# The opening of a fused attention and Mish kernel: first group's maxima first, statistics on ScalarE, input kept whole, keys in two column tiles

## The chip, the cores and the metric

The kernel runs on one core of a Trainium2 chip. A core has TensorE (PE, with its weight loads listed apart as PEld), VectorE (DVE), ScalarE (ACT), GpSimd (POOL) and SyncE (SP), which here only issues DMAs. Every engine works through its own list of instructions in order and waits on semaphores of the others. The metric is the device time of one execution in microseconds (us); lower is better. Before the change it is 1585.07, the median of 3 runs (1584.73 to 1585.38).

## The reference

`x` is 1 x 2048 x 512. It is normalised row by row, then goes two ways, which are multiplied:

```python
xn = (x - mean(x)) / sqrt(var(x) + 1e-5)

# A: attention, 32 query heads of 16, one key head and one value head shared by all
q = (xn @ wq) split into 32 heads; k = xn @ wk; v = xn @ wv      # wk, wv: 512 x 16
p = softmax(q k^T * 16 ** -0.5)
s = concat(p @ v) @ wo

# B: dense, Mish, dense
h = xn @ w1 + b1                                                  # 512 x 1792
g = silu((h * tanh(softplus(h))) @ w2)                            # 1792 x 512

out = x + s * g
```

All arrays are float32.

## The kernel before

The 2048 rows are four *blocks* of 512 (`NC`, `C`), and each block four *tiles* of 128 rows; tile `t` is the `t % 4`-th of block `t // 4`. Products that need float32 accuracy on the fast path are made of three products of high and low parts (`TERMS`): a high part is the value rounded to the engine's fast format, the low part is the rest.

Attention is cut into 32 *units* `v` of 16 *steps*. A unit is four heads with the 512 queries of one block; a step takes one tile of 128 keys against them: four score products (`e`), an exponential each on ScalarE (into `pts`), and four value products (`pv`). The softmax needs the greatest score of every query row beforehand. So for every unit there are also 32 pairs of *maximum products* (`m`; the two of a pair are of two heads, a = 0 and 1, which lie in the upper and the lower 64 rows of PE's array): 128 queries against one block of 512 keys; VectorE reduces each to one column (`mb`). Pair `n` of a unit belongs to key block `n // 8`. When a unit's 32 pairs are done, `c_rows` makes *rows* of them (three small reductions, a 32x32 transpose) and eight DMAs write these rows into the unit's query tile `qt`, where they are subtracted by the score product itself. Unit 0 can therefore give no score before all of its 32 pairs are done, with the keys of all four blocks. The maxima run `LEAD` = 22 steps ahead of the scores: 44 pairs are made before the first score. A query product (`q_group`) makes eight heads, enough for two units; units 0 and 1 come from the first.

Beside the scores PE does the *extra* products (`xps`): the query products, the first dense layer (`m1_group`, from a weight tile `ws`), the second (`m2_groups`, tiles `wb`) and the output (`wo_groups`). Weights come by DMA into one of two *raw* buffers and are split there into high part (ScalarE in the opening, GpSimd later) and low part (GpSimd). The activation between the layers runs on ScalarE and GpSimd.

The *opening* is what stands ahead of the first score. A small planner at the end of the function builds it: tasks with an engine, a guessed duration (`us`), predecessors and a priority are placed one by one, always the one that can start first; where PE has a free moment it gets a pair of maxima ("M"), part of an extra product ("X") or a product that is thrown away (`warm`). The order that it writes down is then fixed for each engine. `E0` is the planner's guess of when the first score starts, and `X_US` how often an extra group may begin. The tasks are, for every block: statistics of its tiles on VectorE (`stats`: BN_STATS, BN_AGGR), the root of the variance (`norm_a` on VectorE, `norm_b` as Ln and Exp on ScalarE, `norm_c` on VectorE; blocks 2 and 3 together), scaling (`x_scale`: VectorE in block 0, ScalarE after), transposing on PE, copying from PSUM, and the product with `wk` and `wv` (`k_proj` into `kp`). Keys are then written to rows 0 to 47 of `ks` as high part (`k_high`, ScalarE) and low part (`k_low`, VectorE), and `k_move` copies them by DMA to rows 64 to 111, because the products of a = 1 read there. Only then can maxima of that block start.

The order of pairs in the opening is a table, `MSEQ`: eight pairs of unit 0, eight of unit 1, the other 24 of unit 0, then unit 1. While the row steps of unit 0 are pending, `m_ready` lets no pair through.

The transposed input of blocks 1 to 3 is split at once (`x_high2` on ScalarE, `x_low2` on GpSimd). Block 1 stays in SBUF, blocks 2 and 3 are stored split in DRAM (`xt_keep`) and come back later in four DMAs (`xt_loads`). Before that, `wbs` and `ot_all` are their homes, so the tiles of the second layer's weights come late.

Of the kernel before, what the change touches and what calls it, by code (L numbers as in the profile page):

```python
# [20 lines left out]
P = 128  # L21
# [14 lines left out]
E0 = 86.0  # L36
X_US = 13.0
# [21 lines left out]
MSEQ = ([(0, n) for n in range(8)] + [(1, n) for n in range(8)]  # L59
        + [(0, n) for n in range(8, 32)] + [(1, n) for n in range(8, 32)])  # L60


def m_need(v):

    return (40, 64)[v] if v < 2 else 32 * (v + 1)
# [59 lines left out]
def block_kernel(ctx: ExitStack, tc: tile.TileContext, x, wq, wk, wv, wo, w1, b1, w2, out):  # L125
# [34 lines left out]
    def pool_at(margin):  # L160
        t = step_of(busy[0]) + margin
        return max(t if lead else math.ceil(2 * t) / 2, step[0])
# [69 lines left out]

    def stats(t):
        st = sb.tile([P, 6], F32, tag="st", name=f"st{t}")
        dve.bn_stats(st, xin[divmod(t, 4)])
        dve.bn_aggr(mvs[:, t], st)

# [6 lines left out]
    def norm_a(z):  # L244
        dve.tensor_scalar(ve[:, z], mvs[:, z, 1], EPS, None, op0=ALU.add)
# [11 lines left out]

    def x_scale(t):
        x_ = xin[divmod(t, 4)]
        if t < 4:  # L260
            dve.tensor_scalar(x_, x_, rstd[:, t:t + 1], nbias[:, t:t + 1], op0=ALU.mult, op1=ALU.add)
        else:
            xn_scale(x_, x_, t)
# [3 lines left out]
    def x_transpose(t):  # L267
        c, tt = divmod(t, 4)
        xp_of[t] = ps_e.tile([P, NDT, P], F32, tag="e", name=f"xp{t}")
        for dt in range(NDT):  # L270
            pe.transpose(xp_of[t][:, dt], xin[c, tt][:, P * dt:P * (dt + 1)], ident)  # L271
# [22 lines left out]
    def x_high2(c, k):  # L294
        act.activation(xt_of[c][:, 0, 2 * k:2 * k + 2], xf_of[c][k], AF.Copy)

    def x_low2(c, k):
        sub(pool, xt_of[c][:, 1, 2 * k:2 * k + 2], xf_of[c][k], f(xt_of[c][:, 0, 2 * k:2 * k + 2]))

# [4 lines left out]

    def k_proj(c, dts):
        if 0 in dts:
            kp_of[c] = ps_v.tile([64, C], F32, tag="v", name=f"kp{c}")
        for dt in dts:
            if c > 0:
                pe.matmul(kp_of[c], wkf[:, dt], xf_of[c][dt // 2][:, dt % 2], start=(dt == 0), stop=(dt == 3))  # L310
                continue
            xt = xt_of[c]
            for i, (a, b) in enumerate(TERMS):
                pe.matmul(kp_of[c], wk3[:, a, dt], xt[:, b, dt], start=(dt + i == 0), stop=(dt == 3 and i == 2))

    def k_high(c):
        act.activation(ks[0:48, C * c:C * (c + 1)], kp_of[c][0:48], AF.Copy)

    def k_low(c):
        cs = slice(C * c, C * (c + 1))  # L320
        sub(dve, ks[0:16, cs], kp_of[c][0:16], f(ks[0:16, cs]))

    def k_move(c):
        cs = slice(C * c, C * (c + 1))
        sp.dma_start(f(ks[64:112, cs]), f(ks[0:48, cs]))

    def v_copy(c):
        vt_of[c] = sb.tile([P, C], F32, tag="xr", name=f"vt{c}", bufs=4)[0:32]
        act.activation(vt_of[c], kp_of[c][32:64], AF.Copy)
# [67 lines left out]

    def arrived(tag):
        k, n = todo[tag]
        if k >= RING[tag] and items[tag][k - RING[tag]].users:  # L400
# [3 lines left out]
    def home(tag, k):  # L404
        if tag == "wx":
            return (xt_of[NC] if k else new_xt(NC))[:, :, k]
        if tag == "wb":
# [38 lines left out]
    def load(tag):  # L446
# [4 lines left out]
        if n == len(its) or lead and tag == "wb" and n and now[0] < kept_at.get(3, 1e9):  # L451
            return
        it = its[n]
        taken = n >= RING[tag] and its[n - RING[tag]].users
        if taken and (tag != "ws" or kept.get(it.key)):
# [442 lines left out]
    def xt_keep(c, h):  # L898

        if h == 0:  # L900
            xt_kept[c] = dram.tile([P, 2, NDT, C], F32, tag=f"xt{c}", name=f"xtk{c}")
        sp.dma_start(xt_kept[c][:, h], f(xt_of[c][:, h]))

    def xt_loads(c, before):
        def part(k):
            if k == 0:
                new_xt(c)
            o = (slice(None), k // 2, slice(2 * (k % 2), 2 * (k % 2) + 2))
            done = sp_at(0.5) + 2
            sp.dma_start(f(xt_of[c][o]), xt_kept[c][o])  # L910
            if k == 3:
                xt_done[c] = math.ceil(done)

        def loads():
            for k in range(4):
                later(1 + 2 * k, lambda k=k: part(k))
# [16 lines left out]
    for c in range(NC):  # L933
        for k in range(3):
            a = take(2)
            if k == 1 and 1 <= c < NC - 1:
# [50 lines left out]
    m_next = [0, 0]  # L987

    def m_one(a, other=False):
        v, n = MSEQ[m_next[a]] if m_next[a] < 64 else divmod(m_next[a], 32)  # L990
# [26 lines left out]
    def c_rows(v):  # L1017
# [18 lines left out]
        def move():  # L1036
# [3 lines left out]
            for a in range(1, -1, -1):  # L1040
                r = 64 * a + 48
                for b in range(4):
                    sp_at(0.68)
                    sp.dma_start(f(q[r:r + 2]).rearrange("o p (t b n) -> b o (p t) n", b=4, n=32)[b],
# [107 lines left out]
    kept_at = {}  # L1152
# [48 lines left out]

    step[0] = (0.0 - E0) / STEP_US
    xat = {t: landed(DMA_US) for t in range(4)}
# [12 lines left out]
    new_xt(1)  # L1216
    tmp = ot_all.rearrange("p a h n -> p (a h) n").rearrange("p (h t) n -> p h t n", h=2)
    xt_of[2] = tmp
    xt_of[3] = wbs[:, 0:4].rearrange("p (h a) b n -> p h (a b) n", h=2)
# [8 lines left out]
    st = [task("DVE", 0.83, lambda t=t: stats(t), at=xat[t], prio=t // 4 * 2) for t in range(16)]  # L1228
    kv_done = None
    for c0, c1 in ((0, 1), (1, 2), (2, 4)):  # L1230
        z = slice(4 * c0, 4 * c1)
        na = task("DVE", 0.2, lambda z=z: norm_a(z), st[z], prio=c0 and 1)
        nb = task("ACT", 0.45, lambda z=z: norm_b(z), [na])
        nrm = task("DVE", 0.8, lambda z=z: norm_c(z), [nb], prio=2 * c0 and 1)
        for c in range(c0, c1):
            xs, his = [], []
            for t in range(4 * c, 4 * c + 4):
# [275 lines left out]
```

## Time and profile before

| what | value |
|---|---|
| time, median of 3 | 1585.07 us |
| profiled execution | 1585.32 us |
| its span | 1583.4 us |
| busy: PE, VectorE, ScalarE, GpSimd | 1566.4, 1342.0, 1295.1, 619.0 us |
| GpSimd busy, 0 to 100 us / 100 to 1500 us | 62.40 / 538.99 us |
| first maximum on VectorE | 30.30 us |
| first score product on PE | 91.19 us |

In the rows of a timeline the first number is the start in us from the span's start, the second the length of the row (several instructions in a row are merged, their number behind the x), then engine, line, operation, result <- operands and shapes; square brackets give idle time of the engine before the row and what ended it. SPq rows are issues of DMAs: their length is the time in which the queue was held by them. Matmuls of several row or column tiles overlap, so the lengths of PE rows can't be added. The granted TensorE clock is 1.00 in the opening and in the stage after it.

### The profile page before, as it was taken

To read this page: it belongs to the slowest core of one execution; us is meant where nothing else is said; L and a number is where in the kernel's file an instruction comes from. 1 tells how busy PE (TensorE), PEld (TensorE's weight loads), DVE (VectorE), ACT (ScalarE), POOL (GpSimd) and SP (SyncE) were. 2 spreads that over 40 slices of the span, in tenths; PEclk is the share of its full clock that TensorE was granted. 3 is DMA by queue.
4 is the path that set the end of the run, shared out by engine and by line. 5 is a ranking of instruction groups with operands and counts; after the bars stand their busy time and mean duration, and the time that the engine had idled before them with its cause. 6 is when DMAs were issued, how large, how long until landed. Compare 5 with 4: busy or idle time off the path is not lost.

```text
span 1583.4 us, 31224 instructions
## 1 busy us (share of the span) xinstructions
PE 1566.4 (99%) x11656; PEld 872.8 (55%) x11656; DVE 1342.0 (85%) x2299; ACT 1295.1 (82%) x2492; POOL 619.0 (39%) x626
## 2 busy tenths in 40 slices
PE   8999999999999999999999999999999999999998
PEld 5445555655555565565555556556555555655643
DVE  7988888888988988888898988888889999888821
ACT  5569889778899788877988888897788978888796
POOL 3788448338256111431624322163152323315021
PEclk9999999999999999999999999999999999999999
DMA  5333133124042215203113220332311213021200
GB/s 163 142 118 124 42 97 117 51 64 165 22 131 64 73 56 164 67 20 102 55 31 109 88 94 17 115 108 78 101 58 59 92 45 114 16 97 32 74 22 27
DMA packets 73542, 127.29 MB, mean 80 GB/s; under 512 B 21488, under 2 KB 35312, under 8 KB 72880
## 3 DMA queue, kind: packets, MB, share of 16 engines
q1 hardware_dynamic: 73392, 125.30, 25.2%
q8 instruction: 92, 1.51, 0.4%
q14 instruction: 58, 0.48, 0.1%
HBM read 76.36 MB, written 27.26 MB: 65 GB/s over the span
## 4 chain that ended last, share of the span: by engine, by line
PE 94%; ACT 2%; DVE 1%; POOL 1%; DMA 1%; SPq 0%; issue 0%; DVEq 0%; ACTq 0%; POOLq 0%
PE xps L118 42%; PE pv L1059 30%; PE m L1001 12%; PE e L973 6%; PE xps L114 2%; ACT pts L978 1%; PE kp L310 1%; DMA rawwb<-in_dram 1%; PE wop L114 0%; DVE mb L1005 0%; PE warm L1292 0%; POOL wbs L171 0%; DMA pts<-in_dram 0%; SPq L1077 0%; PE xp L271 0%
## 5 line engine op out<-in xcount | busy, mean ns | idle before, releaser
L1005 DVE TENSOR_REDUCE mb<-m 128x1 f32<-128x512 f32 x2048 | 1266.1, 681 | 169.9 <-PE m L1001 113.1
L978 ACT ACTIVATE pts<-e 128x512 f32<-128x512 f32 x2042 | 1062.3, 607 | 221.8 <-PE e L973 156.0
L1001 PE MATMUL m<-ks,qt 48*128 48x512 f32 (+1 forms) x2048 | 839.5, 425 | 1.1 <-DVE mb L1005 0.8
L973 PE MATMUL e<-qt,ks 64*128 64x512 f32 x2048 | 748.5, 408 | 1.8 <-ACT pts L978 1.7
L1059 PE MATMUL pv<-pts,vaug 128*32 128x512 f32 x4084 | 531.0, 603 | 0.0
L1001 PEld LDWEIGHTS m<-ks,qt 48*128 48x128 f32 (+1 forms) x2048 | 366.4, 185 | 114.4 <-DVE mb L1005 62.0
L973 PEld LDWEIGHTS e<-qt,ks 64*128 64x128 f32 x2048 | 372.2, 186 | 29.2 <-ACT pts L978 19.0
L118 PE MATMUL xps<-xt,ws 64*128 64x512 f32 x1212 | 336.4, 410 | 0.0
L118 PEld LDWEIGHTS xps<-xt,ws 64*128 64x128 f32 x1212 | 209.0, 185 | 198.4 <-ACT pts L978 130.8
L118 PE MATMUL xps<-wbs,act 64*128 64x512 f32 x1248 | 314.6, 396 | 0.0
L118 PEld LDWEIGHTS xps<-wbs,act 64*128 64x128 f32 x1248 | 225.9, 185 | 66.9 <-ACT pts L978 33.5
L1059 PEld LDWEIGHTS pv<-pts,vaug 128*32 128x32 f32 x4084 | 87.8, 108 | 150.2 <-issue 142.3
L171 POOL TENSOR_TENSOR hb<-hb,t 128x512 f32<-128x512 f32 x56 | 72.1, 1287 | 150.8 <-PE m L1001 76.6
L181 POOL TENSOR_SCALAR t<-t 128x512 f32<-128x512 f32 x56 | 34.4, 614 | 190.1 <-ACT t L739 190.1
L118 PE MATMUL xps<-xt,wq 64*128 64x512 f32 x336 | 93.0, 410 | 0.0
L118 PEld LDWEIGHTS xps<-xt,wq 64*128 64x128 f32 x336 | 58.0, 185 | 55.6 <-ACT pts L978 37.7
L118 PE MATMUL xps<-wbs,ot_all 64*128 64x512 f32 x288 | 79.4, 408 | 0.0
L171 POOL TENSOR_TENSOR oc<-oc,sc 128x512 f32<-128x512 f32 (+1 forms) x16 | 20.6, 1288 | 148.5 <-DMA wbs<-w 71.2
L118 PEld LDWEIGHTS xps<-wbs,ot_all 64*128 64x128 f32 x288 | 49.5, 184 | 46.8 <-ACT pts L978 28.5
L171 POOL TENSOR_TENSOR act<-hb,act 128x512 fp32r<-128x512 f32 x56 | 72.2, 1288 | 4.7
L171 POOL TENSOR_TENSOR hb<-hb,u 128x512 f32<-128x512 f32 x56 | 72.3, 1290 | 4.4
L171 POOL TENSOR_TENSOR u<-u,t 128x512 f32<-128x512 f32 x56 | 72.0, 1285 | 4.7
(122 smaller groups left out, 828.8 us busy)
## 6 DMA issues: line engine op xcount, KB each, us to landing
wbs<-w SPq DMA_DIRECT2D x38, 512.0 KB
ws<-w SPq DMA_DIRECT2D x35, 512.0 KB
qt<-qh SPq DMA_DIRECT2D x256, 32.0 KB
w<-wbs SPq DMA_DIRECT2D x14, 512.0 KB
w<-ws SPq DMA_DIRECT2D x14, 512.0 KB
wq<-wq SPq DMA_DIRECT2D x14, 512.0 KB
wbs<-wo SPq DMA_DIRECT2D x12, 512.0 KB
rawws<-in_dram SPq DMA_DIRECT2D x21, 256.0 KB
```

The lines of the kernel that those rows point to most:

```text
L114: self.pe.matmul(ps, self.lhs(), self.rhs(), start=(self.k == 0), stop=(self.k == self.tot - 1))
L118: i = self.pe.matmul(ps, self.lhs()[o], self.rhs()[o], start=(self.k == 0 and self.halves == 0), stop=(self.k == self.tot - 1 and self.hal ...
L171: eng.tensor_tensor(out=o, in0=a, in1=b, op=op)
L181: pool.tensor_scalar(o, o, lim, 0.0, op0=ALU.min, op1=ALU.max)
L310: pe.matmul(kp_of[c], wkf[:, dt], xf_of[c][dt // 2][:, dt % 2], start=(dt == 0), stop=(dt == 3))
L973: pe.matmul(e, ks[o:o + 64, P * k:P * (k + 1)], q[o:o + 64, p], start=True, stop=True)
L978: x = act.activation(dst, e, AF.Exp, scale=0.25)
L1001: pe.matmul(m, q[o, p, P * t:P * (t + 1)], ks[o, C * kb:C * (kb + 1)], start=True, stop=True)
L1005: return dve.reduce_max(out=mb_of[v][:, kb, z:z + 1], in_=m, axis=AX.X)
L1059: pe.matmul(o[32 * j:32 * j + 32], vaug[:, k], pt, start=(k == 0), stop=(k == 15))
```

## The change

- *Maxima.* The table is gone. The planner keeps a count for either unit and takes the pair that can start first, unit 0 where it is no more than 0.6 us later; pairs may also run while the row steps are pending.
- *Statistics and roots.* The fourth block's four tiles go to ScalarE: one pass sums (`stats_sum`), one squares the difference (`stats_var`). Blocks 1 to 3 each have a root of their own, with `norm_a` and the new `norm_d` (six steps for `norm_c`'s four) on GpSimd.
- *Scaling.* Even tiles go to VectorE (block 0) or GpSimd, odd ones to ScalarE. The fourth transpose of block 0 uses a bank of another PSUM pool.
- *Input.* Blocks 1 to 3 are not split in the opening. They are stored whole in two parts a block, come back in two DMAs and are then split by GpSimd (`halve`). Block 1 is stored too, and its place holds first-layer weights (`xtw`); second-layer weights may be loaded in the opening.
- *Keys.* In blocks 1 to 3 the key product is two products of 256 columns, into partitions 0 to 63 and 64 to 127. `k_high`, `k_low`, `v_copy` and `k_move` are two instructions each.
- *Rows.* In the opening every second one of unit 0's eight row DMAs is issued from ScalarE's queue.

```diff
-E0 = 86.0
-X_US = 13.0
+E0 = 81.0
+X_US = 9.0
...
-MSEQ = ([(0, n) for n in range(8)] + [(1, n) for n in range(8)]
-        + [(0, n) for n in range(8, 32)] + [(1, n) for n in range(8, 32)])
...
+    def stats_sum(t):
+        w = sb.tile([P, D], F32, tag="u", name=f"sq{t}", bufs=2)
+        act.activation(w, xin[divmod(t, 4)], AF.Identity, scale=-1.0 / 8192, accum_out=nms[:, t - 12:t - 11])
+
+    def stats_var(t):
+        w = sb.tile([P, D], F32, tag="t", name=f"sv{t}", bufs=2)
+        act.activation(w, xin[divmod(t, 4)], AF.Square, scale=1.0 / 16, bias=nms[:, t - 12:t - 11],
+                       accum_out=mvs[:, t, 1:2])
...
+    def norm_d(z):
+        r, h = rstd[:, z], hv[:, z]
+        pool.tensor_tensor(out=h, in0=ve[:, z], in1=r, op=ALU.mult)
+        pool.tensor_tensor(out=h, in0=h, in1=r, op=ALU.mult)
+        pool.tensor_scalar(h, h, -0.5, 1.5, op0=ALU.mult, op1=ALU.add)
+        pool.tensor_tensor(out=r, in0=h, in1=r, op=ALU.mult)
...
+        pool.tensor_tensor(out=nbias[:, z], in0=h, in1=r, op=ALU.mult)
+        pool.tensor_scalar(nbias[:, z], nbias[:, z], k, 0.0, op0=ALU.mult, op1=ALU.add)
...
-        if t < 4:
-            dve.tensor_scalar(x_, x_, rstd[:, t:t + 1], nbias[:, t:t + 1], op0=ALU.mult, op1=ALU.add)
+        if t % 2 == 0:
+            (dve if t < 4 else pool).tensor_scalar(x_, x_, rstd[:, t:t + 1], nbias[:, t:t + 1], op0=ALU.mult, op1=ALU.add)
...
+            for i, (w, x_) in enumerate(terms):
+                for o, z, _ in sides(c):
+                    pe.matmul(kp_of[c][o:o + HALF, 0:z.stop - z.start], w, x_[:, z], start=(dt + i == 0),
+                              stop=(dt == 3 and i == len(terms) - 1))
...
+        def halve(n):
+            x_ = xt_of[c]
+            hi_pool(x_[:, 0, n], f(x_[:, 1, n]))
+            sub(pool, x_[:, 1, n], f(x_[:, 1, n]), f(x_[:, 0, n]))
...
-                    sp.dma_start(f(q[r:r + 2]).rearrange("o p (t b n) -> b o (p t) n", b=4, n=32)[b],
+                    (act if lead and b % 2 else sp).dma_start(f(q[r:r + 2]).rearrange("o p (t b n) -> b o (p t) n", b=4, n=32)[b],
```

How this moves instructions is shown at three places. The first is ScalarE's list from the first query product (`qh`) to the first key copy (`ks`), before; `rstd` is the root, `pts` the input tiles, `vt` the values.

```order
L674 ACTIVATE qh0_0_280<-xps_267 128x512
L248 ACTIVATE rstd_98<-ve_105 128x4
L249 ACTIVATE rstd_98<-rstd_98 128x4
L213 ACTIVATE pts_102<-pts_102,nbias_99,rstd_98 128x512 x3
L317 ACTIVATE ks_92<-kp0_299 48x512
L329 ACTIVATE vt0_346<-kp0_299 32x512
```

The same stretch of ScalarE's list now:

```order
L704 ACTIVATE qh0_0_278<-xps_265 128x512
L257 ACTIVATE rstd_98<-ve_106 128x4
L258 ACTIVATE rstd_98<-rstd_98 128x4
L211 ACTIVATE pts_102<-pts_102,nbias_99,rstd_98 128x512 x2
L240 ACTIVATE sq12_329,nms_105<-pts_102 128x512
L340 ACTIVATE ks_92<-kp0_303 48x512
```

One scaling has left the stretch, and the summing pass of tile 12 has come into it.

The second place is VectorE's list behind the last pair of unit 0 (`m0_0_31`, `m0_1_31`), before; `mp` and `cr` are the row steps, `mb1` takes unit 1's maxima.

```order
L1005 TENSOR_REDUCE mb0_408<-m0_1_31_939 128x1
L1024 TENSOR_REDUCE mp0_942<-mb0_408 128x2x8
L1027 TENSOR_REDUCE mp0_942<-mp0_942 128x2x8
L1029 TENSOR_REDUCE mp0_942<-mp0_942 128x2x8
L1034 STREAM_TRANSPOSE cr0_978<-mp0_942 128x32
L1005 TENSOR_REDUCE mb1_551<-m1_0_8_980 128x1
L1005 TENSOR_REDUCE mb1_551<-m1_1_8_983 128x1
```

The same stretch of VectorE's list now:

```order
L1043 TENSOR_REDUCE mb0_399<-m0_1_31_919 128x1
L1062 TENSOR_REDUCE mp0_922<-mb0_399 128x2x8
L1043 TENSOR_REDUCE mb1_807<-m1_0_2_938 128x1
L1043 TENSOR_REDUCE mb1_807<-m1_1_2_941 128x1
L1043 TENSOR_REDUCE mb1_807<-m1_0_3_944 128x1
L1043 TENSOR_REDUCE mb1_807<-m1_1_3_947 128x1
L1065 TENSOR_REDUCE mp0_922<-mp0_922 128x2x8
L1067 TENSOR_REDUCE mp0_922<-mp0_922 128x2x8
L1043 TENSOR_REDUCE mb1_807<-m1_0_4_968 128x1
L1043 TENSOR_REDUCE mb1_807<-m1_1_4_971 128x1
L1043 TENSOR_REDUCE mb1_807<-m1_0_5_974 128x1
L1043 TENSOR_REDUCE mb1_807<-m1_1_5_977 128x1
```

Unit 1 is at its third pair here and not at its ninth, and two groups of two pairs stand between the row steps; the transpose follows, and then six more pairs up to the first score.

The third place is SP's list up to the key moves of the third and fourth block (`ks`), before; `raw...` are weight loads into the two raw buffers, `xtk` the stored input.

```order
L465 DMA rawws2_540<-in_5_dram 128x4x128
L465 DMA rawws3_593<-in_5_dram 128x4x128
L902 DMA xtk2_601<-ot_all_103 128x2048
L325 DMA ks_92<-ks_92 48x512
L902 DMA xtk2_601<-ot_all_103 128x2048
L902 DMA xtk3_698<-wbs_101 128x2048 x2
L325 DMA ks_92<-ks_92 48x512
```

The same stretch of SP's list now:

```order
L495 DMA rawws3_569<-in_5_dram 128x4x128
L497 DMA rawwb2_609<-in_7_dram 128x512
L348 DMA ks_92<-ks_92 48x256 x2
L495 DMA rawws4_691<-in_5_dram 128x4x128
L932 DMA xtk3_720<-xf3_0_672 128x1024
L497 DMA rawwb3_727<-in_7_dram 128x512
L932 DMA xtk3_720<-xf3_1_673 128x1024
L495 DMA rawws5_735<-in_5_dram 128x4x128
L497 DMA rawwb4_778<-in_7_dram 128x512
L348 DMA ks_92<-ks_92 48x256 x2
```

Between the two key moves stand four weight loads where there was none, and the moves are two DMAs each.

225 lines of the change are left out of this document (119 added, 106 removed).

## The prediction

> **What bounds the kernel now.** I read the time by stage first (the windows: busy us of each engine, with counts, then granted clock, DMA share, GB/s), then the timeline of VectorE through the opening, then PE's, ScalarE's, GpSimd's and the SP queue's against it.
>
> ```profile
> core 0: us, PE busy (x) PEld busy (x) DVE busy (x) ACT busy (x) POOL busy (x), PEclk, DMA share, GB/s
> 0.00:100.00 100.00, 90.71 (x390) 50.34 (x390) 87.59 (x171) 53.85 (x102) 62.40 (x67) 1.00 0.43 135
> 100.00:1500.00 1400.00, 1399.62 (x10816) 788.86 (x10812) 1233.60 (x2092) 1176.81 (x2264) 538.99 (x541) 1.00 0.25 79
> ```
>
> From 100 us on PE never stands still. The order of both programs after the opening is the same block for block (442 blocks with the same numbers of score, maximum, value and extra products), but for three whole products of the last opening group, which become six half ones in the first two blocks, where VectorE sets the pace and PE has room for them. So the time moves by what the opening gains or loses, unless GpSimd's new work later holds PE up. The opening does the same 44 pairs of maxima before the first score in both programs. What sets its end is VectorE:
>
> ```profile
> 20.45 0.69 DVE L171 TENSOR_TENSOR ql<-xps,qh 128x512 fp32r<-128x512 f32 x1 [1.95 <-ACT qh L674]
> ...
> 29.36 1.03 DVE L245 TENSOR_SCALAR ve<-mvs 128x8 f32<-128x8 f32 x1
> 30.30 1.27 DVE L1005 TENSOR_REDUCE mb<-m 128x1 f32<-128x512 f32 x2
> 31.50 0.15 DVE L242 SCALAR_TENSOR_TENSOR hv<-ve,rstd 128x8 f32<-128x8 f32 x1
> ...
> 32.17 4.07 DVE L1005 TENSOR_REDUCE mb<-m 128x1 f32<-128x512 f32 x6
> ...
> 40.78 0.21 DVE L337 COPY vaug<-vp 128x64 f32<-128x64 f32 x1
> 40.95 9.60 DVE L1005 TENSOR_REDUCE mb<-m 128x1 f32<-128x512 f32 x14
> ...
> 61.65 0.67 DVE L171 TENSOR_TENSOR ks<-kp,ks 16x512 fp32r<-16x512 f32 x1
> 62.25 3.66 DVE L1005 TENSOR_REDUCE mb<-m 128x1 f32<-128x512 f32 x6
> ...
> 65.97 18.09 DVE L1005 TENSOR_REDUCE mb<-m 128x1 f32<-128x512 f32 x30
> 84.10 0.26 DVE L1024 TENSOR_REDUCE mp<-mb 128x16 f32<-128x64 f32 x1
> ...
> 84.82 0.21 DVE L1034 STREAM_TRANSPOSE cr<-mp 128x32 f32<-128x32 f32 x1
> 88.19 12.05 DVE L1005 TENSOR_REDUCE mb<-m 128x1 f32<-128x512 f32 x20 [3.16 <-PE m L1001]
> ```
>
> A maximum costs 18.09/30 = 0.603 us when they come back to back. The 40th pair ends at 84.10; then the rows are made; 3.16 us are lost; and the 44th pair (eight maxima more) ends at 88.19 + 8 x 0.603 = 93.0. VectorE then stays without a gap through the first scores, so the first steps hang on it:
>
> ```profile
> 43.44 1.07 PE L310 MATMUL kp<-xf,wkf 128*64 128x512 f32 x2
> 44.44 0.50 PE L1001 MATMUL m<-ks,qt 64*128 64x512 f32 x2
> ...
> 84.67 3.06 PE L114 MATMUL xps<-xt,ws 128*128 128x512 f32 x12 [1.30 <-ACT hb L733]
> ...
> 91.19 0.39 PE L973 MATMUL e<-qt,ks 64*128 64x512 f32 x1
> ...
> 99.51 1.06 PE L1059 MATMUL pv<-pts,vaug 128*32 128x512 f32 x8
> ```
>
> I therefore price the change by the end of the 88th maximum: 93.0 now.
>
> **The change, part by part. Start of the maxima.** These rows carry the chain to the first one:
>
> ```profile
> 9.96 1.08 DVE L261 TENSOR_SCALAR pts<-pts,rstd,nbias 128x512 f32<-128x512 f32 x2
> ...
> 10.96 1.49 DVE L261 TENSOR_SCALAR pts<-pts,rstd,nbias 128x512 f32<-128x512 f32 x1
> ...
> 10.72 1.45 POOL L171 TENSOR_TENSOR wq<-rawwq,wq 128x512 fp32r<-128x512 f32 x1
> ...
> 12.83 0.68 DVE L235 BATCH_NORM_STATS2 st<-pts 128x6 f32<-128x512 f32 x1
> ...
> 13.65 1.85 DVE L171 TENSOR_TENSOR xt<-xp,xt 128x512 fp32r<-128x512 f32 x3
> ...
> 16.23 0.66 DVE L171 TENSOR_TENSOR xt<-xp,xt 128x512 fp32r<-128x512 f32 x1
> ...
> 22.70 2.23 ACT L213 ACTIVATE pts<-pts,nbias,rstd 128x512 f32<-128x512 f32 x3 [1.00 <-DVE nbias L242]
> 24.83 0.57 ACT L317 ACTIVATE ks<-kp 48x512 fp32r<-48x512 f32 x1
> ...
> 26.80 0.52 SPq L325 DMA_DIRECT2D ks<-ks  x1
> ...
> 29.22 0.50 PE L1001 MATMUL m<-ks,qt 64*128 64x512 f32 x2
> ...
> 8.25 0.32 POOL L171 TENSOR_TENSOR wk<-wkv,wk 128x64 fp32r<-128x64 f32 x1
> 8.54 0.24 POOL L166 TENSOR_SCALAR wk<-wkv 128x64 fp32r<-128x64 f32 x1
> ```
>
> Block 0 now scales two of four tiles on ScalarE and puts the fourth transpose into a bank of its own. VectorE is through its two at 9.96 + 1.08 = 11.04 instead of 12.9, does two statistics (0.82 each, 12.83 to 13.65) to 12.68 and four low parts (1.85/3 = 0.62) to 15.15, against 16.89 now. ScalarE's side (two scalings at 2.23/3 = 0.74 and four high copies) ends earlier. So the first query product, its high part and ql come 1.74 us earlier, qh ending at 18.7. Then ScalarE, in order: 0.4 for the root, the wait for GpSimd's six small steps, which replace VectorE's four (four of two inputs at 0.32 and two at 0.24: 1.76), two scalings 1.48, the first summing pass 0.74: key copy at 23.1 instead of 24.83. From that copy to the first maximum product it is 29.22 - 24.83 = 4.4, so 27.5, and VectorE starts at 28.0 instead of 30.30. Until then it only waits: the last four statistics, with their root's input (1.03, beside a GpSimd product), are gone. **-2.3** (-3 with GpSimd steps half as long, -1 with twice).
>
> A summing ScalarE pass is not in the trace; the nearest are 0.57 and 0.74, so eight cost 4.6 to 6 us. In blocks 1 to 3 they replace six splits and six scalings on ScalarE; they lie beside the maxima, but each stands ahead of copies that PE waits for (below).
>
> A page speaks against them. Trace: one table load, at the start, beside everything. The Trainium skill, ScalarE: Activation LUTs, "Table sets: the hidden batching unit", says that each change of function set costs about 2.7 us; with squares in another set than Ln and Exp, four there and back would be an estimated 21 us, and the sum a loss. The changed program's order has one load still, so I give it nothing.
>
> **VectorE between.** The normalisation of blocks 2 and 3 goes: 31.50 to 32.17, **-0.7**. Key lows come in halves, six of 16x256 for three of 16x512: between 0.31 and 0.62 each; with 0.21 for 64 elements and 0.60 for 512 I take 0.40 and 0.60 as now: **+0.5** (0 to +1.9).
>
> **Keys in two column tiles.** A block's step is now 1.00 of key product and 0.44 of maxima, 1.44, while VectorE needs 1.21 for the pair. The stretch 30.30 to 84.10 is 53.8, of which 80 x 0.603 = 48.2, the normalisation 0.7, three lows 1.8 and three value copies 0.6: 2.5 lost, most of it there (14 maxima in 9.60, 1.16 over). Eight value products in four column tiles take 1.06 together, so column tiles overlap here; two halves should take 0.5 a step. **-2.5** (0 if they don't).
>
> **After the rows.** Maxima of unit 1 now run between and behind the row steps, which frees VectorE's 3.16: **-3.2**. The same number of maxima is done in all. Row DMAs:
>
> ```profile
> 67.13 10.85 SPq L467 DMA_DIRECT2D rawwb<-in_dram  x2
> 79.59 6.21 SPq L465 DMA_DIRECT2D rawws<-in_dram  x2
> 85.90 5.36 SPq L1044 DMA_DIRECT2D qt<-cr  x8
> ```
>
> Eight issues take 0.67 each and start 0.87 after the transpose, because SP stands in a weight load. Four on ScalarE's queue leave 2.7 a queue. The transpose now has six pairs behind it before the 88th maximum, 7.2 us, longer than issue and landing (2.7 + 2.4, as 26.80 to 29.22). So this part costs and gains nothing; without that cover it would be worth 2.7. ScalarE's four issues stand ahead of a split and three unit steps, 2.7 us late, hidden the same way.
>
> **New waits.** (a) SP: key moves of blocks 2 and 3 now stand behind weight loads that need a raw buffer back from GpSimd. (b) ScalarE's sums and GpSimd's scaling come ahead of the copies that free PE's transposes; PE is in order, so maxima behind them wait. (c) unit 0 has no maxima of another block to go on with. Between 0 and what the same stretch loses now (3.2 + 2.5 = 5.7); I take half, **+2.9**, since each of these chains ends within a few us of its need: the fourth block's key lows stand behind 44 maxima, so near 57.8 (28.0 + 26.5, four lows and three copies 2.2, waits 1.1), their move lands 2.4 later at 60.2, and its first maximum is due behind 52, near 63.7 (28.0 + 31.4, six lows and three copies 3.0, waits 1.3).
>
> **Later.** Blocks 1 to 3 are read back whole and split on GpSimd: four times 0.61 + 1.28 (rows below) a block, 7.6, 23 in all, beside 861 us in which GpSimd is idle from 100 to 1500. Hidden; without cover PE would wait up to 7.6 a block. Storing less and six splits less (1.05 each on ScalarE, 2.40 on GpSimd) lie in the opening beside VectorE.
>
> ```profile
> 31.35 1.05 ACT L295 ACTIVATE xt<-xf 128x1024 fp32r<-128x1024 f32 x1
> ...
> 32.47 2.40 POOL L171 TENSOR_TENSOR xt<-xf,xt 128x1024 fp32r<-128x1024 f32 x1 [2.11 <-ACT xt L295]
> ...
> 79.53 0.61 POOL L181 TENSOR_SCALAR t<-t 128x512 f32<-128x512 f32 x1
> ...
> 80.93 1.28 POOL L171 TENSOR_TENSOR u<-u,t 128x512 f32<-128x512 f32 x1
> ```
>
> Does GpSimd slow VectorE? The third scaling took 1.49 beside GpSimd's 1.45, and 1.03 went to eight numbers at 29.36; thirty maxima beside GpSimd stayed at 0.603. The Trainium skill, GPSIMD Engine Reference, section 1, says that the two share SBUF interfaces, in conflict when VectorE uses two ports or reads two SBUF inputs; the trace agrees. By that rule maxima, which read PSUM, stay free; if they were hit, each GpSimd product of 1.28 would cost VectorE two maxima.
>
> **Sum.** -2.3 - 0.7 + 0.5 - 2.5 - 3.2 + 2.9 = -5.3: the 88th maximum near 87.7. The profiled execution is 1585.3 (span 1583.4 and 1.9 around it), 0.25 above the median: **1580.0**.
>
> **Rivals.** *No new wait*: -8.2, 1577.1; for it, the slack above; against it, three chains that all end close. *Column tiles don't overlap*: -2.8, 1582.5; against it the value products. *A hold takes the gain*: SP is held before the fourth block's keys as long as the two loads at 67.13 held it, 10.85; slack is 3.5, so 7.3 are lost: -8.2 + 7.3 = -0.9, 1584.4. *Slower*: the same hold befalls third and fourth block, 14.6 lost: +6.4, 1591.7. It decides from 11.4 us of waits on. For it, the loads ahead of both moves and GpSimd's queue of products; against it, those long holds happened when nothing behind them was due.
>
> **How the numbers follow.** Forecast 0.60 (its own range 1577.1 to 1582.8, terms with waits of 0 to 5.7); no new wait 0.08; no overlap 0.07; one hold 0.12; slower 0.13. A change of 0.2%, 3.2 us, is about what this kernel's measurement can tell from none: 1581.9 is the border. Faster 0.65 (0.57 + 0.08), same 0.22 (0.03 + 0.07 + 0.12), slower 0.13. Range 1577.0 to 1586.0, from no wait to past the single hold; it leaves out the slower case and a little below.
>
> **What would show it.** Right: first maximum near 28, rows transposed near 79 to 80, no VectorE gap of 3 us behind them, first scores near 85 to 86, key steps of 0.5 under 1.21 pairs, six GpSimd steps near 1.8, the same pace after 100. Wrong: gaps before VectorE's 17th or 25th pair (keys late), PE waiting at transposes of blocks 2 and 3, key halves one after the other, or PE idle at the start of a block.

## The result, and the profile after

The changed kernel takes 1593.26 us (median of 6, 1591.59 to 1595.24), the kernel before 1584.90 beside it: 1.0052 times as long, 95% interval [1.0039, 1.0065], so 8 us slower where 5 us faster were predicted. The profiled execution took 1591.68 us, span 1589.9. The windows by stage, with some stretches of 10 us (columns as in the prediction; the last three are granted clock, DMA share, GB/s):

```profile
0.00:100.00 100.00, 85.64 (x369) 50.18 (x369) 72.52 (x139) 47.98 (x108) 54.76 (x84) 0.93 0.45 134
50.00:60.00 10.00, 9.53 (x32) 5.32 (x33) 6.32 (x12) 4.95 (x11) 8.71 (x14) 0.56 0.21 57
80.00:90.00 10.00, 7.03 (x29) 4.29 (x28) 7.57 (x16) 2.93 (x5) 5.06 (x6) 0.94 0.19 53
90.00:100.00 10.00, 8.91 (x33) 4.31 (x31) 6.58 (x12) 4.68 (x8) 5.42 (x5) 0.89 0.20 55
100.00:1500.00 1400.00, 1399.24 (x10808) 793.99 (x10809) 1237.22 (x2098) 1180.54 (x2269) 566.51 (x569) 1.00 0.24 76
```

VectorE, which should have lost its gaps, is busy 72.52 us of the first 100 instead of 87.59. Behind 100 us PE stands as little as before, although GpSimd works 27.5 us more there. The loss lies whole in the opening: the first score product starts at 99.73 instead of 91.19, 8.5 us later, and the 88th maximum, by which the prediction prices, ends at 101.94 where 87.7 was forecast. Three places make it. The timeline of the start:

```profile
1.99 9.41 PE L1252 MATMUL warm<-qt 128*128 128x512 f32 x30 [1.99 <-DVE one L191]
...
12.50 2.48 DVE L169 TENSOR_TENSOR xt<-xp,xt 128x512 fp32r<-128x512 f32 x4 [0.45 <-ACT xt L303]
...
12.90 4.39 PE L1321 MATMUL warm<-qt 128*128 128x512 f32 x8
13.43 0.19 PEld L1321 LDWEIGHTS warm<-qt 128*128 128x128 f32 x1 [0.37 <-PE warm L1321]
...
17.43 3.04 PE L112 MATMUL xps<-xt,wq 128*128 128x512 f32 x12
...
25.27 0.57 ACT L340 ACTIVATE ks<-kp 48x512 fp32r<-48x512 f32 x1
...
29.72 1.29 DVE L1043 TENSOR_REDUCE mb<-m 128x1 f32<-128x512 f32 x2 [1.70 <-PE m L1039]
30.00 0.65 PE L335 MATMUL kp<-xf,wkf 128*64 128x256 f32 x4
...
31.01 1.08 PE L335 MATMUL kp<-xf,wkf 128*64 128x256 f32 x8
```

The low parts end at 14.98, as predicted, but eight fillers (`warm`, products without use that keep PE busy) stand in front of the query product and take 4.39 us; it begins 2.3 us later than the forecast had it, and the first maximum comes 1.7 us later (29.72 for 28.0). The changed `keep_warm` writes all of these fillers into `ps_x`, a pool of one bank, which is one buffer: each filler waits there until the one before it has ended, as the weight load at 13.43 shows. Before, the nine fillers up to this place took the banks of `ps_m` in turn (the 13 later ones were in `ps_x` too). What costs is the wait for the buffer and not the bank itself: the thirty products at 1.99 write one tile in one bank with no wait between them, and take 0.31 us each. The list of the change ahead of the prediction does not name this line. The key steps, eight half products, do take 1.08 for two: the tiles overlap. The timeline of the third block:

```profile
43.11 0.53 SPq L495 DMA_DIRECT2D rawws<-in_dram  x1
...
46.45 0.63 ACT L449 ACTIVATE xtw<-rawws 128x512 fp32r<-128x512 f32 x1 [4.06 <-DMA rawws<-in_dram]
46.99 0.75 ACT L340 ACTIVATE ks<-kp 48x256 fp32r<-48x256 f32 x2
...
48.55 0.86 DVE L169 TENSOR_TENSOR ks<-kp,ks 16x256 fp32r<-16x256 f32 x2 [2.98 <-ACT vt L353]
...
49.73 0.69 ACT L763 ACTIVATE hb<-xps,b1c 128x512 f32<-128x512 f32 x1
...
50.47 0.50 PE L1321 MATMUL warm<-qt 128*128 128x512 f32 x1 [3.92 <-ACT hb L763]
...
51.54 1.15 SPq L348 DMA_DIRECT2D ks<-ks  x2
...
57.93 1.29 DVE L1043 TENSOR_REDUCE mb<-m 128x1 f32<-128x512 f32 x2 [0.48 <-PE m L1039]
59.70 1.29 DVE L1043 TENSOR_REDUCE mb<-m 128x1 f32<-128x512 f32 x2 [0.48 <-PE m L1039]
```

ScalarE waits 4.06 us for a weight load that SP issues late, at 43.11; its split stands in the list ahead of the key copy and of the copy `hb`, for which PE's next filler waits: 3.92 us. After that the granted clock is 0.56 and pairs come every 1.77 us instead of 1.21. The timeline of the end:

```profile
77.70 16.44 SPq L495 DMA_DIRECT2D rawws<-in_dram  x4
80.43 0.63 ACT L449 ACTIVATE xtw<-rawws 128x512 fp32r<-128x512 f32 x1 [4.90 <-DMA rawws<-in_dram]
...
81.69 1.66 PE L112 MATMUL xps<-xt,xtw 128*128 128x512 f32 x6 [1.53 <-ACT hb L763]
...
88.47 2.48 DVE L1043 TENSOR_REDUCE mb<-m 128x1 f32<-128x512 f32 x4 [1.88 <-PE m L1039]
90.87 0.20 DVE L1072 STREAM_TRANSPOSE cr<-mp 128x32 f32<-128x32 f32 x1
91.75 0.63 ACT L449 ACTIVATE xtw<-rawws 128x512 fp32r<-128x512 f32 x1 [4.76 <-DMA rawws<-in_dram]
...
94.23 2.76 SPq L1082 DMA_DIRECT2D qt<-cr  x4
...
99.73 0.39 PE L1010 MATMUL e<-qt,ks 64*128 64x512 f32 x1
```

Four weight loads go one by one, SP is in them for 16.44 us, and the row DMAs behind them start 3.2 us after the transpose. ScalarE's splits wait for each load, PE for ScalarE's copies behind the splits, VectorE for PE. The four row DMAs on ScalarE's queue stand behind these splits and end even later than SP's, at 97.58 against 96.99.

### The profile page after: what moved, and what is told of

It reads as the page before. It is cut to its first block, busy times and chain, and to the rows that moved or that the text cites. A ratio compares the mean times of both kernels' runs of the same rounds, so it can differ in the third digit from the quotient of the medians.

```text
span 1589.9 us, 31336 instructions
## 1 busy us (share of the span) xinstructions
PE 1567.2 (99%) x11680; PEld 881.2 (55%) x11680; DVE 1335.8 (84%) x2282; ACT 1297.4 (82%) x2512; POOL 638.9 (40%) x671
## 4 chain that ended last, share of the span: by engine, by line
PE 94%; ACT 2%; DVE 1%; DMA 1%; POOL 1%; issue 0%; SPq 0%; DVEq 0%; POOLq 0%; ACTq 0%
PE xps L116 42%; PE pv L1097 31%; PE m L1039 11%; PE e L1010 6%; PE xps L112 1%; ACT pts L1015 1%; DVE mb L1043 1%; PE warm L1252 1%; PE warm L1321 0%; DMA rawwb<-in_dram 0%; PE wop L112 0%; PE xp L294 0%; SPq L722 0%; DMA rawws<-in_dram 0%; DMA rawwq<-in_dram 0%
## 5 line engine op out<-in xcount | busy, mean ns | idle before, releaser
L116 PE MATMUL xps<-xt,ws 64*128 64x512 f32 x1122 | 311.4, 410 | 0.2 <-ACT pts L1015 0.2
L116 PEld LDWEIGHTS xps<-xt,ws 64*128 64x128 f32 x1122 | 193.3, 185 | 182.2 <-ACT pts L1015 121.3
```

What stands on the lines that cost most here:

```text
L116: i = self.pe.matmul(ps, self.lhs()[o], self.rhs()[o], start=(self.k == 0 and self.halves == 0), stop=(self.k == self.tot - 1 and self.hal ...
```

## The experiments

The theories named below. A: weight loads and their splits stand in the in-order lists of SP and ScalarE ahead of what the maxima need, and wait for SP or for one of two raw buffers. B: the lower granted clock after a pause of PE is a large part of the loss. C: the fillers' single bank, that is, single buffer. D: the new order of maxima itself. E: a gain in the opening is given back later. F: the lists are simply too long.

| run | what | first maximum | first score | median us | ratio to before, 95% |
|---|---|---|---|---|---|
| before | | 30.3 | 91.19 | 1584.90 | |
| after | | 29.7 | 99.73 | 1593.26 | 1.0052 [1.0039, 1.0065] |
| e1 | three banks | 27.9 | 94.22 | 1588.95 | 1.0022 [1.0013, 1.0032] |
| e2 | no second-layer loads | 29.1 | 93.78 | 1588.94 | 1.0021 [1.0012, 1.0031] |
| e3 | true arrival | 29.6 | 103.22 | 1596.11 | 1.0067 [1.0052, 1.0082] |
| e4 | e1, e2, e3 | 26.6 | 86.16 | 1590.43 | 1.0031 [1.0020, 1.0041] |
| e5 | e1, pause filled | 27.2 | 94.07 | 1587.88 | 1.0020 [1.0010, 1.0029] |
| e6 | e1, split behind keys | 27.7 | 97.84 | 1591.15 | 1.0039 [1.0024, 1.0054] |
| e7 | e6, fifth weight later | 28.2 | 97.90 | 1590.92 | 1.0041 [1.0027, 1.0055] |
| e8 | before, column tiles | 30.4 | 97.26 | 1588.75 | 1.0021 [1.0012, 1.0031] |
| e9 | after, five buffers | 31.8 | 98.65 | 1589.83 | 1.0028 [1.0015, 1.0040] |
| e10 | e9, three banks | 27.4 | 91.74 | 1584.92 | 0.9996 [0.9986, 1.0005] |
| e11 | e10, split behind keys | 26.9 | 87.27 | 1581.87 | 0.9980 [0.9971, 0.9990] |
| e12 | before, five buffers | 29.8 | 90.67 | 1584.77 | 0.9999 [0.9990, 1.0008] |
| e13 | e8, five buffers | 30.2 | 92.05 | 1582.34 | 0.9980 [0.9970, 0.9989] |
| e14 | e11, rows on SP alone | 26.4 | 87.51 | 1583.02 | 0.9981 [0.9972, 0.9991] |
| e15 | e11, one bank | 29.5 | 99.97 | 1586.72 | 1.0000 [0.9991, 1.0010] |
| e16 | e11, statistics on VectorE | 27.6 | 90.16 | 1585.63 | 1.0001 [0.9992, 1.0010] |

The first two numbers of a row are of its one profiled execution. That was the longest of the row's executions in e3, e8, e9, e12 and e15 (1593.87 us in e9, 1593.25 in e15) and the shortest in e5, so these first scores are late or early examples and not typical ones.

### The three holds one by one

e1 gives the fillers three banks. It goes further than back to the kernel before: the later fillers, too, leave the extra bank.

```diff
-    def keep_warm():
+    def keep_warm(ps=ps_m, tag="m"):
...
-        ps, tag = (ps_m, "m") if waiting else (ps_x, "x")
```

> Only the fillers ahead of the first query product change: three banks in turn again, as before the change, instead of the single extra bank. Theory A+B (splits of weights that stand in ScalarE's list ahead of key copies and wait for their loads, and the lower granted clock that follows PE's pause): the first query product begins near 15.2 us instead of 17.43 and the first maximum near 27.5 to 28.2 instead of 29.72, but the third block's load is still waited for at about 46.4, so most of the 2 us is lost again there: 1590 to 1592 us against 1593.3 for the changed kernel. Theory C (the fillers themselves are the price): all of the 2.3 us arrive at the end, 1590.5 to 1591.2. Both leave it slower than before; what tells them apart is whether the first score product moves (99.73 now).

Both theories expected too little: 4.3 us. The groups of PE to 110 us tell why, here the fillers of the changed kernel (instructions, busy us and mean ns, then idle time of PE ahead of them and what ended most of it):

```profile
L1321 PE MATMUL warm<-qt 128*128 128x512 f32 x19 | 9.3, 491 | 5.4 <-ACT hb L763 4.7
```

and those of e1:

```profile
L1320 PE MATMUL warm<-qt 128*128 128x512 f32 x19 | 7.5, 456 | 0.2
```

The extra bank also holds the first dense layer's sums until ScalarE has copied them (`hb`). Fillers in it wait for that copy, and PE, in order, with them: the single bank costs at the start and again in the blocks.

e2 leaves the second-layer weights 1 to 4 to later.

```diff
-        if n == len(its):
+        if n == len(its) or lead and tag == "wb" and n:
```

> The second-layer weights 1 to 4 are not loaded in the opening, so that no raw buffer is held by one whose split stands late in ScalarE's list; all else is as in the changed kernel. Theory A: the last first-layer loads go two at a time, the row DMAs are no longer held on SP until 94.23, PE's waits for ScalarE's copies after 80 us (1.53, 1.44 and 0.81) and VectorE's gaps there (1.88, 1.07, 1.61) mostly go: 3 to 5 us faster than the changed kernel, 1588.3 to 1590.3. Rival D (the order of the maxima itself leaves VectorE with nothing to do behind the row steps): the gaps stay and the time is within 1 us of 1593.3.

Theory A, with 4.3 us. The row DMAs start 0.1 us behind the transpose's end, and PE's waits for `hb` behind 80 us are 1.6 in all. The third block is as in the changed kernel, its clock 0.50.

e3 lets the planner count SP's queue and the raw buffers; e4 is e1, e2 and e3 together.

```diff
-    lead["arrive"] = lambda: (landed(DMA_US) - E0) / STEP_US - 0.9
+    def arrive():
+        T["SP"] = max(T["SP"], now[0]) + 0.45
+        return (max(landed(DMA_US), T["SP"] + 2.4) - E0) / STEP_US - 0.9
+    lead["arrive"] = arrive
...
             T["SP"] = max(T["SP"], raw_free.pop(0))
```

> Only the planner's estimate of when a weight load has landed changes: it counts SP's queue and the time at which GpSimd gives the raw buffer back, so the split of the third first-layer weight stands behind the third block's key copy in ScalarE's list. Theory A+B: PE's pause of 3.92 us near 46.5 to 50.5 goes, the granted clock between 50 and 60 us is 1.00 instead of 0.56, the pairs there come at 1.21 instead of 1.77 us, and the time falls by 4 to 7 us to 1586 to 1589. Theory C or D: the pairs recover but the first scores come as late as now, within 1.5 us of 1593.3.

> The three edits together: fillers in three banks, no second-layer weights 1 to 4 in the opening, and true arrival times in the planner. Theories A, B and C together: the first score product near 91 or earlier and a time of 1581 to 1586, so at most as slow as before. Rival D: not below 1588.

e3 was a miss: 2.9 us slower between the medians, though the intervals overlap. PE's pause of 3.92 us becomes one of 1.55 (the clock from 50 to 60 us is 0.60 even so), but the list it makes has fillers in the one bank between the last pairs, and its profile shows them at a granted clock of 0.50:

```profile
88.77 0.80 PE L1330 MATMUL warm<-qt 128*128 128x512 f32 x1 [2.43 <-ACT hb L768]
...
90.65 5.06 PE L1330 MATMUL warm<-qt 128*128 128x512 f32 x6
...
96.47 2.48 DVE L1048 TENSOR_REDUCE mb<-m 128x1 f32<-128x512 f32 x4 [3.66 <-PE m L1044]
96.79 5.06 PE L1330 MATMUL warm<-qt 128*128 128x512 f32 x6
```

Six fillers of 0.84 us each keep VectorE waiting 3.66 us, twice. e4 has the opening that the prediction described, with the first score at 86.16, and is slow all the same: theory E. Its timeline behind the opening:

```profile
86.16 0.50 PE L1015 MATMUL e<-qt,ks 64*128 64x512 f32 x1
...
104.89 6.31 SPq L502 DMA_DIRECT2D rawwb<-in_dram  x2
...
124.78 0.60 SPq L727 DMA_DIRECT2D qt<-ql  x1
...
126.93 0.46 PE L1044 MATMUL m<-ks,qt 64*128 64x512 f32 x1 [2.27 <-DMA qt<-ql]
```

The second-layer loads that were put off now stand on SP ahead of the next unit's query moves. From the first score to the end of the span e4 takes 1499.6 us, 7.4 more than before. The wait is 2.27 of it; the granted clock, 0.71 from 90 to 100 and 0.91 from 120 to 140 us, is worth 2.9 and 1.8 by an estimate that takes PE's time to go with it; the rest is open.

### The clock by itself

e5 is e1 with ten fillers put into PE's pause ahead of the third block's value transposes and five into the next one.

```diff
     def v_transpose(c):
+        if c == 2:
+            more(10)
...
+        if t == 12:
+            more(5)
```

> As the run with fillers in three banks (1588.95), plus ten useless products ahead of the third block's value transposes and five ahead of the fourth block's first transpose, where PE stood for 2.45 and 1.35 us; nothing that is waited for comes earlier. Theory B (the pause lowers the granted clock, and the low clock then costs about 3 us): the granted clock from 50 to 60 us is near 1.00 instead of 0.51, pairs there come at 1.21 to 1.3 instead of 1.76 us, the first score product moves from 94.2 to 91 to 92, and the time is 1585.5 to 1587.5. Rival (the pause alone is the price, the clock follows something else): the clock stays near 0.5 and the time within 1 us of 1588.95, or up to 1 us above it.

PE's pause of 2.45 us in e1, and the window behind it:

```profile
47.40 0.41 PE L358 MATMUL vp<-ident,vt 32*128 32x32 f32 x4 [2.45 <-DVE ks L169]
...
50.00:60.00 10.00, 8.65 (x36) 4.88 (x34) 6.58 (x11) 5.71 (x13) 7.80 (x10) 0.51 0.18 52
```

and of e5:

```profile
50.00:60.00 10.00, 9.84 (x52) 5.30 (x50) 8.20 (x15) 5.71 (x13) 7.93 (x9) 1.00 0.20 61
```

The pause does lower the clock, and VectorE works 1.62 us more when it doesn't. But the first score stays where it was (94.07) and the time falls by no more than it is uncertain: SP still stands in the last four loads to 89.85, and what is won ahead of them is waited for there. Theory B falls as the main cause at this place.

### Where the holds really are

e6 is e1 with the third weight's split behind the third block's copies; e7 puts off the fifth second-layer weight as well.

```diff
         k, n = todo[tag]
+        if lead and tag == "ws" and k == 2 and 2 not in vt_of:
+            return False
```

> As the run with fillers in three banks, and the third first-layer weight is split on ScalarE only behind the third block's key and value copies. Theory A: PE's pauses of 2.45 and 1.35 us go and with them the low clock at 50 to 60; the first score product comes near 88 instead of 94.2. Second-layer weights are still loaded in the opening, so the query moves of the next units are not late: 1582 to 1585, at most as slow as before. Rival E (a gain in the opening is lost again after it, as in the run with all three edits, whose first score came at 86.16 but whose time was 1590.4): 1588 to 1591.

> As the run before it in this set, but the last second-layer weight of the opening (the fifth), whose load keeps a raw buffer until its split late in ScalarE's list, is not loaded in the opening. Theory A: the last first-layer loads go two at a time, the row DMAs are not held on SP, and the clock does not fall at 90 to 100: first score near 86 and 1580 to 1583, so faster than before by 2 to 5 us. Rival E: first score near 86 and 1586 to 1590.

Both misses. With the split moved, PE waits later, here in e6:

```profile
77.02 0.63 ACT L451 ACTIVATE xtw<-rawws 128x512 fp32r<-128x512 f32 x1 [4.25 <-DMA rawws<-in_dram]
77.56 0.58 ACT L710 ACTIVATE qf<-xps 128x512 f32<-128x512 f32 x1
...
78.19 2.93 PE L112 MATMUL xps<-xt,xtw 128*128 128x512 f32 x6 [4.41 <-ACT qf L710]
```

The same hold in another place: the split of another weight waits for its load, and now a query copy stands behind it. So the place in ScalarE's list isn't the cause alone; the loads are. That can be tried without touching a list: e9 is the changed kernel with the same instructions in the same order on every engine, but the opening's raw weights rotate through five tiles, of which three (`y1` to `y3`) are free until later. e10 adds the three banks, e11 the split behind the keys, and e12 is the control.

```diff
-            r = sb.tile([P, D], F32, tag="raw", name=f"raw{tag}{n}", bufs=RAWS)
+            i = nraw[0] % 5
+            nraw[0] += 1
+            if lead and i > 1:
+                r = sb.tile([P, D], F32, tag=f"y{i - 1}", name=f"raw{tag}{n}", bufs=1)
+            else:
+                r = sb.tile([P, D], F32, tag="raw", name=f"raw{tag}{n}", bufs=RAWS)
```

> The changed kernel with the same instructions in the same order on every engine; only the raw weights of the opening rotate through five buffers (three that are otherwise idle until later) instead of two, so that SP's loads no longer wait for a buffer. Theory A (the two raw buffers and what stands behind them in SP's and ScalarE's lists): the third first-layer weight, issued at 43.11, is issued near 39 and its split no longer stands in front of the key copies, PE's pause of 3.92 us goes, the four loads from 77.70 to 94.14 are issued at once, the row DMAs follow the transpose directly, and the first score comes 4 to 7 us before 99.73: 1586 to 1589.5. Rival F (the lists themselves, the order of maxima, fillers and copies, are too long): the holds on SP go, but the first score moves by less than 1.5 us, 1592 to 1593.5.

> The same five raw buffers with the fillers in three banks. Theory A plus the fillers' 2 to 3 us: first score near 89 to 91 and 1582 to 1585, level with the kernel before. Rival F: first score as with three banks alone, 94.2, and 1588 to 1589.

> Five raw buffers, three banks, and the third weight's split behind the third block's key copies (with two buffers: first score at 97.84, 1591.15 us, since PE waited 4.4 us for a query copy that stood behind two splits waiting for their loads). Theory A: those waits go, the first score comes at 86 to 88, 1579.5 to 1583, the first version that beats the kernel before. Rival E (a gain in the opening is lost after it): first score at 86 to 88 and 1585 to 1590. Rival F: first score above 92.

> The kernel before with the five raw buffers, as the control. There SP stood in loads too (10.85 and 6.21 us), but with nothing due behind them but the row DMAs, 0.87 us late: 0 to 1.5 us faster, 1583 to 1585. If it gains 3 us or more, the buffers are a gain of their own and not the reason for the change's loss.

e9 is 3.4 us faster than the changed kernel. One expectation was wrong: the third weight is issued at 45.18 even so, because twelve query moves stand ahead of it on SP; that hold is one of the queue and not of the buffer, so it takes the moved split (e11) to be rid of it. e10 is level with the kernel before and e11 beats it, by 3.2 us (0.20%). The control gains nothing: before, nothing that is due stands behind those loads. The timeline of e11:

```profile
12.45 2.38 PE L1328 MATMUL warm<-qt 128*128 128x512 f32 x8
...
43.29 0.86 DVE L169 TENSOR_TENSOR ks<-kp,ks 16x256 fp32r<-16x256 f32 x2 [0.43 <-ACT vt L353]
...
77.62 0.20 DVE L1080 STREAM_TRANSPOSE cr<-mp 128x32 f32<-128x32 f32 x1
...
77.90 2.80 SPq L1090 DMA_DIRECT2D qt<-cr  x4
...
87.27 0.39 PE L1018 MATMUL e<-qt,ks 64*128 64x512 f32 x1
```

Eight fillers take 2.38 instead of 4.39, the third block's key lows come 5.3 us earlier, the rows leave 0.1 us behind the transpose's end. In ratios to before the three edits make 0.24, 0.32 and 0.16%, one added upon the other, together 0.72% or 11.4 us from 1593.26: the whole loss and the gain. Theory F falls, and D as the cause of the loss: e10 has the changed kernel's order of maxima pair for pair and is level with the kernel before. The third step is less clean than the first two: its edit leads the planner to other lists, with all pairs of unit 0 ahead of the first of unit 1, and the intervals of e10 and e11 overlap a little, so the 0.16% are of the moved split and of this order together.

### Single parts of the change

e8 is the kernel before with the column tiles alone (`sides`, two instructions each in `k_high`, `k_low`, `v_copy`, `k_move`, and the planner's guesses of their times), e13 the same with five buffers.

> The kernel before, with the keys of blocks 1 to 3 in two column tiles and nothing else of the change. The prediction's term: key steps of 0.58 instead of 1.00 between pairs, up to 2.5 us earlier less 0.5 for the key lows in halves: 1582.6 to 1584.9 against 1584.9. Rival (the halves' copies and moves, two for one on ScalarE, VectorE and SP, cost as much as the overlap gives, or the opening ends by another chain): 1584.5 to 1586.5.

> The kernel before with column tiles alone (1588.75 us; its row DMAs stood 8.15 us behind the transpose, in weight loads on SP) and the five raw buffers. If those loads are the loss: row DMAs within 1 us of the transpose at 85, first score near 91 instead of 97.26, 1583 to 1585.5. If the halves' doubled copies and moves are the loss: first score near 95 to 97 and 1587 to 1589.

Alone the tiles lose 0.21% (4.2 us between the medians), with the buffers they win 0.20% (3.0 us; the buffers alone, in e12, won nothing). The end of the opening in e8:

```profile
85.16 0.21 DVE L1041 STREAM_TRANSPOSE cr<-mp 128x32 f32<-128x32 f32 x1
88.08 5.15 SPq L472 DMA_DIRECT2D rawws<-in_dram  x2
...
97.26 0.76 PE L980 MATMUL e<-qt,ks 64*128 64x512 f32 x1 [3.15 <-DMA qt<-cr]
```

and in e13:

```profile
83.50 0.21 DVE L1047 STREAM_TRANSPOSE cr<-mp 128x32 f32<-128x32 f32 x1
83.78 5.35 SPq L1057 DMA_DIRECT2D qt<-cr  x8
...
92.05 0.39 PE L986 MATMUL e<-qt,ks 64*128 64x512 f32 x1
```

The rows leave 7.9 us behind the transpose's end in e8 (two loads ahead of them on SP) and 0.1 in e13: theory A once more. The first score of e13 is no earlier than before's, though; its gain comes behind it (its 33rd score product starts at 114.3 us, before's at 115.5), and by what is open.

e14, e15 and e16 take one part each back out of e11: the row DMAs all on SP, the fillers in the one bank, and the fourth block's statistics on VectorE (`bn_stats`, as blocks 1 to 3).

> The fastest version so far (five buffers, three banks, split behind the keys: 1581.87) with all eight row DMAs on SP. The prediction gave the second queue nothing, since six pairs of maxima stand behind the transpose: 1581 to 1583. If the rows are what the first score waits for: the issue takes 5.4 instead of 2.8 us and the time is 1584 to 1585.

> The fastest version so far with the fillers in the single extra bank again, as in the changed kernel. Theory C: the first query product begins 2 to 2.5 us later and all of it arrives, and fillers wait for copies of the same bank in the blocks: 1584 to 1587. Rival: the later start is absorbed behind the rows, 1581.5 to 1583.

> The fastest version so far with the fourth block's statistics on VectorE (bn_stats, as blocks 1 to 3) instead of eight passes of ScalarE. The prediction: VectorE waits between 21 and 27 us in any case, so its four more statistics (3.3 us) are hidden, and ScalarE's sums cost nothing either: 1581 to 1583. If the sums hold key copies on ScalarE: 1579 to 1581. If the statistics push the maxima back: 1583 to 1585.5.

The second queue is worth nothing (0.9981 and 0.9980), as predicted. The one bank costs 0.20%, 3.2 us, here too, with the same instructions in the same order on every engine. From e9 to e15, both with the one bank, the split behind the keys and the lists that follow from it are worth 0.28%. The statistics were a miss on the cheap side: on VectorE they cost 0.21%, 3.3 us. In e16's profile PE waits 1.34 us for a scaling of GpSimd at 31.34, and then the clock falls:

```profile
30.00:40.00 10.00, 8.66 (x39) 5.55 (x40) 7.15 (x14) 7.20 (x19) 5.31 (x8) 0.64 0.53 170
40.00:50.00 10.00, 9.95 (x45) 4.63 (x43) 6.55 (x12) 4.82 (x13) 3.07 (x3) 0.68 0.60 203
```

The first maximum stands at 27.57 there, 0.6 later than in e11, so the statistics themselves were nearly hidden. What they moved in the planner's lists, and the clock, are left as causes; no run separates the two.

## Why the prediction was wrong

- *Start of the maxima, -2.3:* it became -0.6. The chain to the low parts (14.98 for 15.15) and GpSimd's six small steps (21.58 to 23.19, 1.6 for 1.76) were priced well. What was missing is a line of the change that had no term: the fillers' single bank. Without it the first maximum is at 26.4 to 28.2, where 28.0 was forecast.
- *VectorE between, -0.7 and +0.5:* right; two key lows take 0.86.
- *ScalarE's table, nothing:* right; both traces have one table load, at the start, and it takes 1.28 us.
- *Column tiles, -2.5:* right in mechanism, 0.54 us a step. Their worth alone is -3.0 us (e13) or +4.2 (e8), by what SP holds; but in e13 the 88th maximum comes only 1.1 us earlier than before (91.94 for 93.06), so the 3.0 are not the term's chain alone.
- *After the rows, -3.2, and the row DMAs, 0:* the second queue is indeed worth nothing (e14), but VectorE's gap came back as four of 1.88, 1.07, 1.61 and 0.74 us, since PE waited.
- *New waits, +2.9 (0 to 5.7):* the step that failed. The first score came 8.5 us late where the sum had 5.3 early, 13.8 us of waits. The term was taken from what the opening lost before; it should have been read from the lists. (a) SP: weight loads did hold the key moves, by 2.1 us in the third block (51.54 behind 49.41) and 1.1 in the fourth, but PE waited for these no more than 0.16 us. What cost were the row DMAs behind four loads, and the third load, late behind query moves. (b) ScalarE: not the sums but the weight splits stood ahead of the copies, which I had not priced. In time, one edit added upon the other, the buffers take back 3.4 us, the bank 4.9 and the split with its new lists 3.1. So the waits that the term was meant for come to 6.5 us, above its upper end, and the bank's 4.9 stood in no term.
- *Later, hidden:* right for the changed kernel (PE busy 1399.24 of 1400). In e4, where loads moved behind the opening, SP there was not free.
- *The measure:* the first score tells the time to about 2 us in most kernels. From it to the end of the span it is 1492.2 us before, 1490.2 after and 1490 to 1494 in most others, but 1488.4 in e13, 1495.8 in the profiled execution of e12 and 1499.6 in e4.
- *The rivals:* the slower one, 1591.7 with a chance of 0.13, came within 2 us of the result. Its mechanism, in-order lists behind weight loads, was at work, but at other places, and 4.9 us of the loss are the fillers, which it doesn't know: that the number is so near is luck. Against it I had put that the long holds of SP "happened when nothing behind them was due". The control e12 shows that this is true before, and that's why it was no argument: the change puts something due behind them.

With the three holds gone the change comes within 2 us of the sum, 1581.87 us against 1580.0. Its terms are not all as forecast: in e11 the first maximum (26.95) and the transpose (77.62) come earlier than the 28 and the 79 to 80 of the prediction, the first score (87.27) later than its 85 to 86, so part of the agreement is luck.

## What to carry to other kernels

Where a change lets one chain run earlier, read what stands ahead of its steps in every in-order list, loads and their buffers first: a wait that cost nothing sits there until something due stands behind it. Before a part is judged by a run, make sure that such a hold doesn't decide the run: column tiles measured +4 or -3 us by the number of raw buffers. And see where work without use writes; a filler must never need a buffer that real work, or the filler before it, releases.

## What the runs showed of the hardware

- *Products one after the other.* Fillers of 128x512 take 0.55 us each where each waits for the end of the one before (4.39 for eight, in a pool of one buffer), 0.30 where the pool's buffers alternate (2.38 for eight), and 0.31 into one bank without a wait between them (9.41 for thirty). At a granted clock of 0.50, with the wait, it is 0.84 (5.06 for six).
- *The clock falls after short pauses too.* The Trainium skill, TensorE: Matmul & The Clock Gate, Part 1, gives an idle window of about 3.4 us as what lowers the clock. The 3.92 us pause here, followed by 0.56, agrees; but e1 shows 0.51 after a pause of 2.45 us with one of 1.35 behind it, and e16 0.64 around one of 1.34. Nor does the length of a pause alone decide: one of 1.55 in e3 is followed by 0.60, and one of 1.56 left e11 at 1.00. The same part of the Trainium skill tells of a second failure mode, micro-idles between groups of products; whether that is at work here, and where the border lies, no run here shows.
- *What goes with a low clock.* The ten executions of e11 go from 1579.8 us at a mean granted clock of 1.000 to 1584.2 at 0.997, with 1584.1 at 0.995; those of e15 from 1582.9 at 0.999 to 1593.2 at 0.992. So the same program has a lower clock in some executions than in others. It is not the only thing that varies: executions of the kernel before took 1584.4 and 1587.4 us, both at 1.000.
- *A summing pass on ScalarE* takes 0.61 us and 0.18 for a second instruction that reads the accumulator, one that squares and sums 0.72 and 0.20.
